# Attention and MoE on one core: turned-back products at 256 columns and an event table by name

## The chip, the cores and the metric

The kernel runs on one core of a Trainium2 chip. The metric is the time of one execution on the device, in microseconds; the median of several executions counts. The engines that matter here are TensorE (PE, with its weight loads shown apart as PEld), VectorE (DVE), ScalarE (ACT), GpSimd (POOL) and the queue of SyncE (SP), which issues most transfers.

## What is computed

Eight batches of eight heads go through rotary attention (576 positions, head width 64), and the 4608 resulting rows of width 512 go through a layer of eight experts of which each row uses one. All data are float32.

```python
q_rot, k_rot = rotate(q), rotate(k)              # B, H, S, D = 8, 8, 576, 64
scores = q_rot @ k_rot.T / sqrt(D)
attn = exp(scores - max(scores))
x = (attn / (sum(attn) + 1e-9)) @ v              # then heads side by side: 4608 x 512
e_idx = argmax(x @ w_gate); gate_w = softmax(x @ w_gate)[e_idx]
eom = sigmoid(x @ w_output_gate)
out[rows of e] = gate_w * eom[e] * (relu(x @ w1[e]) @ w2[e])
```

## The kernel before

**The pairs.** Two heads of one batch make a pair, four pairs a batch, 32 pairs in all. A pair takes nine steps; its step number is g = 9n + k for pair n. The raw and rotated queries and keys are split in a high and a low part (POOL multiplies, adds and subtracts, ACT rounds), because scores are made of three products each: high by high, high by low, low by high. The table UNITS puts the nine score tiles of a pair on five of its steps: tiles 0 and 1 on step 0, 2 and 3 on step 2, tile 4 (the last 64 queries of both heads, block-diagonal, `bd`) on step 4, 5 and 6 on step 5, 7 and 8 on step 7. In a unit of two, the first tile belongs to one head and the second to the other, so one reads the upper 64 partitions and the other the lower 64.

**A tile's way.** TensorE makes the scores of a tile (L496, six products). VectorE takes the maximum (L501), ScalarE the exponential with its sum (L514), VectorE turns the result in blocks of 32 (L521, 1152 columns for two tiles). After the last tile, the values are multiplied (L542, in the four pieces av0 to av3 of PIECES, spread between the score units of the next pair) and summed in the PSUM tile `acc`. ScalarE copies `acc` out (L549 to L551), TensorE multiplies it back into token rows by a matrix that holds the identity and the gate weights (`back`, L557, 160 columns for each of five chunks of tokens), and `divide` scales by one over the softmax sum into the row buffer `xb`: three VectorE operations (L565, L567, L570) and two ScalarE ones (L574). The score tiles hold two buffers of two PSUM banks, `acc` the other four banks; `acc` has one buffer. So av0 of a pair can start when `divide` of the pair before it has read `acc`.

**The order.** It is written by hand. EVENTS gives each event a step, counted from the pair's first, and a sub-slot within the step; `step` (L339) emits scores, maxima and exponentials of the step's unit and then the events of sub-slots 1, 2 and 3. Each engine runs its instructions in the order in which they are emitted. After the fourth pair of a batch, `place` spreads the routing of the batch's 576 tokens over the following 38 steps (offset PLACE = 20): sums of the logits (L603), the rank product (L682, L683: which place in its expert's list each token gets) into a free corner of `acc`, its readers on VectorE (L687 and the next), one-hot rows (L713 on VectorE, L715 on POOL), the list product (L723) into a corner of `acc` and its addition to the lists (L726), and three row stores from `xb` to `xd` in memory (L665, L667).

**The transfers.** SP issues the loads of queries and keys (`raw`, L426, two for a pair), of the values (`v`, L433: four of 32 partitions each for a pair, the same memory four times), the row stores and the weight loads (`wr`, L984). A load waits on its queue until the last reader of its buffer is done.

**The second part.** Slots of expert rows follow: gather (L971), turn (L1009), first product (L1023, L1031), second product (L1074), scatter. Slot 0's weights are loaded, and its first products made, while the last pairs still run.

## Time and profile before

| | us |
|---|---|
| median of three runs | 1078.68 |
| lowest and highest | 1078.12 and 1080.76 |
| the profiled execution | 1082.95 |
| its span, first to last instruction | 1081.0 |
| TensorE busy in the span | 995.4 |
| VectorE busy | 836.2 |
| ScalarE busy | 627.4 |
| GpSimd busy | 585.5 |

The profiled execution is 4.3 us longer than the median, and 1.9 us of it lie around the span. Times within the trace are microseconds from the span's start. The granted clock is the share of TensorE's full speed that the chip allowed in a stretch. "Idle before" is the time in which an engine stood still just ahead of an instruction, and the name behind the arrow is what ended last of what it waited for; "issue" means that nothing in the profile was waited for. TensorE overlaps products of its queue, so that a run of products is best read by the times at which they start.

### The profile page before, as it was taken

The numbers are of one execution on the slowest core, as the hardware profiler recorded it, in microseconds if no ns is written. First come the engines' busy times: TensorE is split into PE (matmuls) and PEld (weight loads), VectorE is DVE, ScalarE is ACT, GpSimd is POOL, SyncE is SP. The second block draws the span as 40 slices with busy tenths as digits, with TensorE's granted clock in tenths as the row PEclk, the third lists the DMA queues.
The fourth block names the chain that finished last, engine by engine and source line by source line (L and its number), as shares of the span: only waits on it lengthen the run. The fifth ranks groups of instructions, "written<-read, shape, count | busy, mean of one in ns | idle before, by whom it ended". The sixth has DMA issues, their size and how long they took to land.

```text
span 1081.0 us, 34609 instructions
## 1 busy us (share of the span) xinstructions
PE 995.4 (92%) x14465; PEld 864.7 (80%) x14465; DVE 836.2 (77%) x1364; ACT 627.4 (58%) x1318; POOL 585.5 (54%) x540
## 2 busy tenths in 40 slices
PE   4999999989999899999778999999999999999995
PEld 3888777777777777777667888889898898899984
DVE  6789898978989888887875787666867857767782
ACT  4566656646656565564444455545865856757762
POOL 5676796867968679586531242213542443542621
PEclk9999999989999998898889999999999999999998
DMA  6755574655746556455256597766977977888860
GB/s 196 191 149 139 159 215 119 174 141 152 209 115 183 158 137 198 113 162 149 52 162 200 181 340 220 248 214 203 342 231 265 325 261 266 310 300 280 270 254 28
DMA packets 59760, 216.47 MB, mean 200 GB/s; under 512 B 9453, under 2 KB 11596, under 8 KB 55504
## 3 DMA queue, kind: packets, MB, share of 16 engines
q1 hardware_dynamic: 51920, 194.41, 58.5%
q0 software_dynamic: 6496, 18.92, 4.9%
q8 instruction: 115, 1.88, 0.7%
q10 hardware_dynamic: 1184, 0.89, 0.3%
q14 instruction: 45, 0.37, 0.1%
HBM read 196.04 MB, written 20.24 MB: 200 GB/s over the span
## 4 chain that ended last, share of the span: by engine, by line
PE 73%; DVE 14%; issue 6%; ACT 3%; DMA 2%; POOL 1%; ACTq 0%; DVEq 0%; POOLq 0%
PE py L1074 17%; PE acc L542 17%; PE sc L496 16%; PE ph L1031 14%; PE ph L1023 5%; DVE m L501 4%; DVE pt L521 3%; DVE wl L995 2%; PE mtp L1009 1%; PE acc L557 1%; ACT pm L514 1%; DVE xb L565 1%; ACT xb L574 1%; PE acc L723 1%; PE htp L1059 1%
## 5 line engine op out<-in xcount | busy, mean ns | idle before, releaser
L514 ACT ACTIVATE pm<-sc,m 128x576 f32<-128x576 f32 x288 | 211.0, 737 | 191.3 <-DVE m L501 188.8
L995 DVE TENSOR_TENSOR wl<-wr,wh 128x1024 fp32r<-128x1024 f32 x183 | 254.4, 1402 | 50.5 <-ACT wh L993 48.7
L501 DVE TENSOR_REDUCE m<-sc 128x1 f32<-128x576 f32 x288 | 205.7, 748 | 74.8 <-PE sc L496 73.8
L542 PE MATMUL acc<-pt,v 32*64 32x128 f32 (+1 forms) x9216 | 213.9, 311 | 32.1 <-ACT xb L574 11.1
L496 PE MATMUL sc<-kh,q 64*128 64x288 f32 x1024 | 210.3, 332 | 21.2 <-ACT q L412 10.9
L542 PEld LDWEIGHTS acc<-pt,v 32*64 32x64 f32 x9216 | 171.2, 139 | 57.7 <-issue 28.8
L993 ACT CAST wh<-wr 128x1024 fp32r<-128x1024 f32 x208 | 212.7, 1051 | 5.9 <-DMA wr<-in_w 5.9
L1074 PE MATMUL py<-wh,ht 128*128 128x512 f32 x640 | 214.7, 400 | 0.0
L496 PEld LDWEIGHTS sc<-kh,q 64*128 64x128 f32 x1024 | 150.0, 195 | 54.6 <-ACT pm L514 27.1
L521 DVE STREAM_TRANSPOSE pt<-pm 128x1152 f32<-128x1152 f32 x128 | 174.6, 1364 | 0.0
L438 POOL TENSOR_TENSOR raw<-raw,rt 128x1152 f32<-128x1152 f32 x62 | 163.9, 2643 | 0.3
L1031 PE MATMUL ph<-xt,wh 128*128 128x256 f32 x896 | 161.6, 282 | 2.3 <-DVE xt L1012 1.0
L1031 PEld LDWEIGHTS ph<-xt,wh 128*128 128x128 f32 x896 | 138.5, 189 | 5.3 <-DVE xt L1012 1.9
L496 PE MATMUL sc<-kl,q 64*128 64x288 f32 x512 | 139.9, 304 | 0.0
L1074 PEld LDWEIGHTS py<-wh,ht 128*128 128x128 f32 x640 | 120.4, 188 | 24.0
L1031 PE MATMUL ph<-xt,wl 128*128 128x256 f32 x448 | 125.8, 281 | 0.0
L1074 PE MATMUL py<-wl,ht 128*128 128x512 f32 x320 | 125.1, 391 | 0.0
L995 POOL TENSOR_TENSOR wl<-wr,wh 128x1024 fp32r<-128x1024 f32 x25 | 62.0, 2480 | 111.4 <-ACT wh L993 97.6
L496 PEld LDWEIGHTS sc<-kl,q 64*128 64x128 f32 x512 | 96.8, 196 | 0.0
L442 POOL TENSOR_TENSOR raw<-raw 128x576 f32<-128x576 f32 x62 | 88.0, 1420 | 3.0
L420 POOL TENSOR_TENSOR kl<-raw,kh 128x576 fp32r<-128x576 f32 x31 | 43.7, 1411 | 81.7 <-ACT kh L412 72.1
L1031 PEld LDWEIGHTS ph<-xt,wl 128*128 128x128 f32 x448 | 84.6, 189 | 0.0
(247 smaller groups left out, 1358.7 us busy)
## 6 DMA issues: line engine op xcount, KB each, us to landing
wr<-in_w SPq DMA_DIRECT2D x208, 512.0 KB, 5.5
v<-in_v SPq DMA_DIRECT2D x128, 288.0 KB, 5.9
raw<-in_qk SPq DMA_DIRECT2D x62, 576.0 KB, 4.9
xd<-xb SPq DMA_DIRECT2D x16, 513.0 KB, 6.7
xd<-xb SPq DMA_DIRECT2D x8, 128.2 KB, 4.8
raw<-in_qk SPq DMA_DIRECT2D x2, 288.0 KB, 4.2
rt<-in_rope ACTq DMA_DIRECT2D x2, 288.0 KB, 4.0
raw<-in_qk SPq DMA_DIRECT2D x1, 320.0 KB, 6.7
```

The lines of the kernel that those rows point to most:

```text
L438: self.eng(eng).tensor_tensor(out=rv, in0=rv, in1=self.rt[:, 2 * t:2 * t + 2, x], op=ALU.mult)
L442: self.eng(eng).tensor_tensor(out=r[:, 2 * t, x], in0=r[:, 2 * t, x], in1=r[:, 2 * t + 1, x], op=ALU.add)
L496: nc.tensor.matmul(self.ps[i][:, a, :HS], st, mv, start=(n == 0), stop=(n == 2))
L501: nc.vector.tensor_reduce(self.m[i], ps[:, :, :HS], axis=AX.XY, op=ALU.max, negate=True)
L514: nc.scalar.activation(pe.rearrange("p (a b) -> p a b", a=2), self.ps[i][:, :, :HS], AF.Exp, bias=self.m[i], scale=1.0, accum_out=self.z[: ...
L521: self.nc.vector.transpose(out=self.pt[:, st[0]:st[0] + 6:5, :], in_=pe)
L542: nc.tensor.matmul(self.acc[h * D:h * D + D, a, o:o + 32 * n], self.v[r, h, j, :], self.pt[r, u:u + n, 32 * j:32 * j + 32], start=(j == 0) ...
L993: self.nc.scalar.copy(wh, r)
L995: eng.tensor_tensor(out=wl, in0=r, in1=wh.bitcast(F32), op=ALU.subtract)
L1023: nc.tensor.matmul(ph[:, 0, :], st[:, dc, 0:P], mv[:, dc, :], start=(n == 0), stop=(n == 11))
L1031: nc.tensor.matmul(ph[:, f, :], st[:, dc, fs], mv[:, dc, :], start=(n == 0), stop=(n == 11))
L1074: self.nc.tensor.matmul(py[h], st[:, f, hs], mv, start=(f == 0 and n == 0), stop=(f == 7 and n == 2))
```

## The change

Seven things change.

- **Score tiles in order.** OVER goes from 2 to 0: the second tile's six products follow the first tile's six, where before its first two were interleaved with the first tile's last two.
- **back and divide.** The five products of `back` lie at a spacing of 256 columns in three of `acc`'s banks, where before chunk c lay in bank c modulo 4. `divide` is then two VectorE operations over all five chunks; the third VectorE operation and both of ScalarE's go. The rank product and the list product go to the fourth bank, right behind `back` and ahead of the next scores; their readers on VectorE stand right behind `divide`.
- **den.** The copy of the last chunk's reciprocal goes from VectorE to POOL, and a memset of the row buffer's unused rows goes.
- **The event table.** EVENTS and the new PLACES name each step's place one by one; `step` has a sub-slot before the scores and one between scores and maxima. The query's low part and `lasts` come earlier; the rank product moves by two steps, one-hot rows are spread over steps 44 to 53 of the batch's last pair, the row stores over steps 45, 51 and 56 (before 51, 53 and 54).
- **Loads.** `raw` becomes two tiles. `v` is laid out in memory four times over, so that one transfer fills a head's 128 partitions: two of 576 KB for a pair where four of 288 KB stood. A POOL memset of one column stands ahead of the query load and of the second `v` load, so that these wait for their place in POOL's order.
- **Row stores.** Those of the last batch but one go into the list that the second part works off, and the last batch's go to the end of it.
- **Slot buffers.** At the end of attention only the first weight block of slot 0 is loaded at once, three more follow step by step, the gather of slot 1 comes later, and the turning buffers of the second part get four PSUM banks where they had two.

The diff, cut to its core:

```diff
-PIECES = ((0, 5), (5, 9), (9, 14), (14, 18))
-PLACE, PM = 20, 4
+BS = 256
+EVENTS = {
+    "load1": (-21, 3), "load0": (-16, 2), "mult1": (-11, 3), "add1": (-10, 1), "mult0": (-9, 0), "kh": (-9, 4),
+    "kl": (-6, 3), "add0": (-7, 2), "qh": (-4, 0), "ql": (-4, 2), "lasts": (-3, 2), "loadv0": (5, 4),
+    "loadv1": (6, 1), "av0": (12, 3), "av1": (13, 4), "av2": (14, 2), "av3": (17, 0), "den": (16, 0),
+    "evict": (17, 0), "newxb": (12, 4), "back": (18, 2), "divide": (18, 3),
+}
+PIECES = ((0, 5), (5, 9), (9, 13), (13, 18))
...
-UNITS, OVER = {0: (0, 1), 2: (2, 3), 4: (4,), 5: (5, 6), 7: (7, 8)}, 2
+UNITS, OVER = {0: (0, 1), 2: (2, 3), 4: (4,), 5: (5, 6), 7: (7, 8)}, 0
...
+        moe.load(3, 1)
         for u in range(1, 3):
             moe.split(u)
         att.rest(lambda g: g <= att.G + 8)
-        for j in range(2):
-            moe.products(0, j)
+        moe.products(0, 0)
         moe.first(0, 0)
+        att.rest(lambda g: g <= att.G + 10)
+        moe.products(0, 1)
         moe.first(0, 1)
...
+    small.move(turns, pool(ctx, "ps_y", 2, space=PSUM, side="left", reuse_waits="tile"))
...
+                        if b == nb - 2 and name in ("t0", "t1", "t2"):
+                            self.late.append(fs[name])
...
+            if self.n > 1:
+                self.nc.gpsimd.memset(self.raw[0][:, 0, 0:1], 0.0)
+        self.nc.sync.dma_start(out=self.raw[t], in_=self.qkd[:, 2 * t:2 * t + 2, :])
...
-        for a in (2 * t, 2 * t + 1):
-            self.nc.sync.dma_start(out=self.v[32 * a:32 * a + 32], in_=self.vd)
+        else:
+            self.nc.gpsimd.memset(self.v[:, t, 0, 0:1], 0.0)
+        self.nc.sync.dma_start(out=self.v[:, t, :, :], in_=self.vd[:, t, :, :])
...
-        V.tensor_scalar(rz[0:D, 9:10], rz[D:P, 8:9], 1.0, 0.0, op0=ALU.mult, op1=ALU.add, accum_out=no[0:D])
+        self.nc.gpsimd.tensor_copy(rz[0:D, 9:10], rz[D:P, 8:9])
...
+        self.bk = self.acc.rearrange("p a b -> p (a b)")
         for c in range(NCH):
-            n, o = (P, PO) if c < 4 else (QR, PO + BW)
-            self.nc.tensor.matmul(self.acc[0:n, c % 4, o:o + BW], self.ac[:, c, :, :].rearrange("p a x -> p (a x)")[:, 0:n],
+            n = P if c < 4 else QR
+            self.nc.tensor.matmul(self.bk[0:n, c * BS:c * BS + BW], self.ac[:, c, :, :].rearrange("p a x -> p (a x)")[:, 0:n],
...
-        V.tensor_tensor(out=heads(xb[:, 0:4, x0:x0 + P], D), in0=heads(acc[:, :, PO:PO + P], D),
-                        in1=r4.broadcast_to((P, 4, 2, D)), op=ALU.mult)
...
-        for h in range(2):
-            nc.scalar.activation(xb[0:QR, 4, x0 + h * D:x0 + h * D + D], last[:, h * D:h * D + D], AF.Copy,
-                                 scale=rz[0:QR, 8 + h:9 + h])
+        five = self.bk[:, 0:NCH * BS].rearrange("p (c x) -> p c x", c=NCH)
+        V.tensor_tensor(out=heads(xb[:, :, x0:x0 + P], D), in0=heads(five[:, :, 0:P], D), in1=r.broadcast_to((P, NCH, 2, D)), op=ALU.mult)
+        V.tensor_tensor(out=heads(xb[:, :, l0:l0 + 2 * HL], HL), in0=heads(five[:, :, P:BW], HL),
+                        in1=r.broadcast_to((P, NCH, 2, HL)), op=ALU.mult)
...
-        rk = T["rk"] = psum(2, 2, (NCH + 1) * E).rearrange("p (a b) -> p a b", b=E)
+        rk = T["rk"] = psum(2, 3, (NCH + 1) * E).rearrange("p (a b) -> p a b", b=E)
...
-        T["ls"] = psum(4, 1, lists.shape[1])
+        T["ls"] = psum(4, 3, lists.shape[1])
...
-    vl = np.ascontiguousarray(vr.reshape(nb, NP, 2, NB, 32, D).transpose(0, 1, 4, 2, 3, 5))
+    vl = np.ascontiguousarray(np.tile(vr.reshape(nb, NP, 2, NB, 32, D).transpose(0, 1, 4, 2, 3, 5), (1, 1, 4, 1, 1, 1)))
```

**TensorE at the first scores of pair 11** (`sc11` are its score tiles, `acc9` the tile in which pair 9 is turned back, `acc10` that of pair 10, whose values come next; L682 and L683 make the rank product of batch 1). Before:

```order
L496 MATMUL sc11_2_3270<-kl11_3029,q11_3081 128x288
L496 MATMUL sc11_3_3271<-kh11_3028,q11_3081 128x288
L496 MATMUL sc11_2_3270<-kh11_3028,q11_3081 128x288
L496 MATMUL sc11_3_3271<-kl11_3029,q11_3081 128x288
L496 MATMUL sc11_3_3271<-kh11_3028,q11_3081 128x288 x2
L496 MATMUL sc11_3_3271<-kl11_3029,q11_3081 128x288
L496 MATMUL sc11_3_3271<-kh11_3028,q11_3081 128x288
L682 LDWEIGHTS oneb_103
L682 MATMUL acc9_2987<-ohs1_3159,oneb_103 128x48
L683 LDWEIGHTS trib_102
L683 MATMUL acc9_2987<-ohb1_3155,trib_102 128x40
L542 MATMUL acc10_3298<-pt10_2922,v10_3152 64x160
```

After, from the products of `back` (L593) on:

```order
L593 MATMUL acc9_2974<-ii_102,ac9_3211 128x160 x4
L593 MATMUL acc9_2974<-ii_102,ac9_3211 64x160
L713 LDWEIGHTS oneb_104
L713 MATMUL acc9_2974<-ohs1_3130,oneb_104 128x48
L714 LDWEIGHTS trib_103
L714 MATMUL acc9_2974<-ohb1_3126,trib_103 128x40
L531 MATMUL sc11_2_3263<-kh11_2945,q11_3064 128x288
L531 MATMUL sc11_2_3263<-kl11_2946,q11_3064 128x288
L531 MATMUL sc11_2_3263<-kh11_2945,q11_3064 128x288 x2
L531 MATMUL sc11_2_3263<-kl11_2946,q11_3064 128x288
L531 MATMUL sc11_2_3263<-kh11_2945,q11_3064 128x288
L531 MATMUL sc11_3_3264<-kh11_2945,q11_3064 128x288
```

The rank product went from between the scores and the values to behind `back`; the scores of tile 2 end before those of tile 3 begin.

**VectorE at the same place** (`m` are the maxima of score tiles, `xb2` the row buffer). Before:

```order
L521 STREAM_TRANSPOSE pt10_2922<-pm10_7_3178 128x2x576
L565 TENSOR_TENSOR xb2_2944<-acc9_2987,rz1_117 128x4x128
L567 TENSOR_TENSOR xb2_2944<-acc9_2987,rz1_117 128x4x32
L570 TENSOR_TENSOR xb2_2944<-acc9_2987,rz1_117 64x32
L501 TENSOR_REDUCE m11_2_3285<-sc11_2_3270 128x1
L501 TENSOR_REDUCE m11_3_3288<-sc11_3_3271 128x1
L687 TENSOR_TENSOR pr1_3293<-acc9_2987,base1_3230 128x40
```

After:

```order
L556 STREAM_TRANSPOSE pt10_2910<-pm10_7_3162 128x2x576
L603 TENSOR_TENSOR xb2_2724<-acc9_2974,rz1_118 128x5x128
L604 TENSOR_TENSOR xb2_2724<-acc9_2974,rz1_118 128x5x32
L718 TENSOR_TENSOR pr1_3260<-acc9_2974,base1_3216 128x40
L719 TENSOR_TENSOR cnt_105<-acc9_2974,cnt_105 128x8
L536 TENSOR_REDUCE m11_2_3278<-sc11_2_3263 128x1
L536 TENSOR_REDUCE m11_3_3281<-sc11_3_3264 128x1
```

Two operations read the turned-back products where three did, and the rank product's readers (`pr1`, `cnt`) went from behind two maxima to ahead of them.

**SP's queue while the row stores of batch 1 are issued** (pairs 12 and 13 are being worked; `rk` and `rq` are the two tiles of `raw`). Before:

```order
L433 DMA v11_3461<-in_v 32x2304 x4
L426 DMA raw14_3560<-in_qk 128x1152 x2
L433 DMA v12_3769<-in_v 32x2304 x2
L665 DMA xd_83<-xb1_1726 128x2x513
L433 DMA v12_3769<-in_v 32x2304 x2
L665 DMA xd_83<-xb1_1726 128x2x513
L426 DMA raw15_3860<-in_qk 128x1152
L667 DMA xd_83<-xb1_1726 64x513
L426 DMA raw15_3860<-in_qk 128x1152
L433 DMA v13_4070<-in_v 32x2304 x4
```

After:

```order
L468 DMA v11_3435<-in_v 128x1152 x2
L460 DMA rk14_3441<-in_qk 128x1152
L696 DMA xd_83<-xb1_1513 128x2x513
L460 DMA rq14_3587<-in_qk 128x1152
L468 DMA v12_3738<-in_v 128x1152
L696 DMA xd_83<-xb1_1513 128x2x513
L468 DMA v12_3738<-in_v 128x1152
L460 DMA rk15_3746<-in_qk 128x1152
L698 DMA xd_83<-xb1_1513 64x513
L460 DMA rq15_3887<-in_qk 128x1152
L468 DMA v13_4039<-in_v 128x1152 x2
```

The three stores were one load apart and are now two loads apart, and the load of a pair's values went from four pieces to two, which no longer stand side by side.

## Rows read from the trace of the kernel before

**Rows 1.** The page: busy time of TensorE, and its granted clock in 40 slices.

```profile
PE 995.4 (92%) x14465; PEld 864.7 (80%) x14465; DVE 836.2 (77%) x1364; ACT 627.4 (58%) x1318; POOL 585.5 (54%) x540
...
PEclk9999999989999998898889999999999999999998
```

**Rows 2.** Busy times by stretch, one pair each: length, PE, PEld, DVE, ACT, POOL, clock, DMA.

```profile
63.68:78.86 15.18, 14.50 (x354) 12.32 (x353) 13.47 (x23) 9.93 (x28) 10.85 (x7) 1.00 0.56 141
...
190.35:206.47 16.12, 14.71 (x356) 12.45 (x355) 13.83 (x27) 10.04 (x29) 13.10 (x15) 1.00 0.54 137
206.47:225.48 19.01, 16.43 (x357) 13.60 (x355) 15.48 (x33) 10.30 (x29) 18.54 (x19) 0.91 0.75 205
225.48:244.95 19.47, 18.13 (x356) 15.19 (x355) 15.35 (x26) 9.71 (x28) 9.11 (x9) 0.82 0.46 123
```

**Rows 3.** Busy times by stretch: one batch, four, the last; the passage; the experts.

```profile
141.09:206.47 65.38, 60.07 (x1417) 50.02 (x1416) 58.35 (x109) 39.96 (x111) 52.61 (x57) 1.00 0.60 164
206.47:481.18 274.71, 252.56 (x5662) 210.82 (x5661) 234.02 (x433) 160.17 (x441) 210.31 (x225) 0.94 0.58 159
481.18:564.20 83.02, 69.71 (x1412) 57.42 (x1410) 64.14 (x134) 38.10 (x106) 43.80 (x57) 0.86 0.46 125
...
564.20:640.00 75.80, 67.47 (x683) 58.99 (x675) 53.73 (x113) 35.72 (x57) 22.73 (x21) 0.98 0.68 230
640.00:1045.00 405.00, 402.51 (x2653) 365.45 (x2653) 296.03 (x378) 258.44 (x368) 150.30 (x92) 1.00 0.80 271
```

**Rows 4.** Timeline at a divide: start, length, instruction, idle before and releaser.

```profile
66.31 0.65 DVE L565 TENSOR_TENSOR xb<-acc,rz 128x512 f32<-128x512 f32 x1
66.88 0.28 DVE L567 TENSOR_TENSOR xb<-acc,rz 128x128 f32<-128x128 f32 x1
67.08 0.17 DVE L570 TENSOR_TENSOR xb<-acc,rz 64x32 f32<-64x32 f32 x1
...
67.34 0.51 ACT L574 ACTIVATE xb<-acc,rz 64x64 f32<-64x64 f32 x2 [1.26 <-DVE xb L570]
...
67.90 1.64 PE L542 MATMUL acc<-pt,v 32*64 32x160 f32 x80 [0.68 <-DVE m L501]
```

**Rows 5.** Timeline of TensorE: first and last scores of tile 4, and of two tiles.

```profile
69.47 0.40 PE L496 MATMUL sc<-kh,bd 128*128 128x288 f32 x1
...
70.23 0.29 PE L496 MATMUL sc<-kh,bd 128*128 128x288 f32 x1
...
74.86 0.40 PE L496 MATMUL sc<-kh,q 64*128 64x288 f32 x1
...
76.24 0.28 PE L496 MATMUL sc<-kh,q 64*128 64x288 f32 x1
```

**Rows 6.** Waits of TensorE from 60 to 564 us: total us, times, longest.

```profile
PE acc L542 <- ACT xb L574: 10.4, 14, 1.5
PE acc L542 <- issue: 8.3, 7, 2.6
PE acc L542 <- PE acc L683: 5.1, 7, 0.7
...
PE acc L682 <- DVE m L501: 4.9, 7, 0.7
PE acc L542 <- DVE lists L726: 4.1, 6, 1.0
```

**Rows 7.** Timeline of TensorE: the second longest wait called issue.

```profile
219.68 0.77 PE L542 MATMUL acc<-pt,v 32*64 32x160 f32 x22 [1.81 <-issue]
```

**Rows 8.** Transfers: times issued, KB each, median us from issue to landing.

```profile
v<-in_v SPq DMA_DIRECT2D x128, 288.0 KB, 5.9
...
xd<-xb SPq DMA_DIRECT2D x16, 513.0 KB, 6.7
```

**Rows 9.** Timeline of POOL and of SP's queue in the pair of rows 4.

```profile
72.89 1.41 POOL L420 TENSOR_TENSOR q<-raw,q 128x576 fp32r<-128x576 f32 x1 [0.92 <-ACT q L412]
...
77.90 1.26 SPq L433 DMA_DIRECT2D v<-in_v  x3
```

More of the change, by code (lines that the diff above doesn't have):

```diff
@@ L197, in body @@
         moe.begin0()
+        for u in range(1, 3):
+            att.at(att.G + u - 1, 3, lambda u=u: moe.load(u, 1))
     for g in range(att.G, att.G + TURN):
@@ L200, in body @@
     scores.close()
-    small.move(pool(ctx, "ps_x", 2, space=PSUM, side="right", reuse_waits="tile"))
+    turns = pool(ctx, "ps_x", 2, space=PSUM, side="right", reuse_waits="tile")
+    small.move(turns)
     moe.ph = pool(ctx, "ps_h", 1, space=PSUM, side="right", reuse_waits="tile")
@@ L270, in __init__ @@
         self.go = px.tile([P, 1], F32, name="go")
-        self.last = []
+        self.last, self.late = [], []
         at = self.at
@@ L276, in newxb @@
             xbs[b] = px2.tile([P, NCH, RW], F32, tag="xb", name=f"xb{b}")
-            nc.gpsimd.memset(xbs[b][QR:P, NCH - 1, DM:], 0.0)
         for n, pr in enumerate(self.pairs):
@@ L292, in __init__ @@
                 fs[f"av{k}"] = lambda pr=pr, b0=b0, b1=b1: [pr.values(j) for j in range(b0, b1)]
-            for name, o, k in EVENTS:
+            for name, (o, k) in EVENTS.items():
+                if name in AFTER and g + EVENTS["back"][0] >= self.G:
+                    o, k = AFTER[name]
                 if n > 1 or name not in ("load1", "load0", "mult1", "add1", "kh", "kl", "mult0", "add0", "qh", "ql")[:10 if n == 0 else 2]:
@@ L299, in __init__ @@
                     self.last = fs
[L300 to L304 removed]
+                    for k, f in enumerate(self.late):
+                        self.last.insert(LATER + 2 * k, f)
+                else:
+                    for name, (o, k) in PLACES.items():
+                        if b == nb - 2 and name in ("t0", "t1", "t2"):
+                            self.late.append(fs[name])
                         else:
[L306 removed]
+                            at(g + o, k, fs[name])
     def done(self, b):
[L310 removed]
+        return 9 * (NP * b + NP - 1) + max(o for o, _ in PLACES.values()) + 2
     def at(self, g, k, f):
@@ L341, in step @@
         n, k = divmod(g, 9)
-        if g < G:
-            pr = pairs[n]
-            if k == 0:
-                pr.begin()
-            if k in UNITS:
-                pr.scores(UNITS[k])
-                pr.room(k)
-                for i in UNITS[k]:
-                    pr.peak(i)
-                    pr.exp(i)
-        self.now(g, 1)
+        self.now(g, 0)
+        unit = UNITS.get(k, ()) if g < G else ()
+        pr = pairs[n] if g < G else None
+        if pr and k == 0:
+            pr.begin()
+        if unit:
+            pr.scores(unit)
+        self.now(g, 1)
+        if unit:
+            pr.room(k)
+            for i in unit:
+                pr.peak(i)
+                pr.exp(i)
+        self.now(g, 2)
         if k in TURNS and 0 <= TURNS[k] + 9 * n < G:
@@ L355, in step @@
             pairs[i // 9].turn(i % 9)
-        self.now(g, 2)
         self.now(g, 3)
+        self.now(g, 4)
 class Pair:
@@ L973, in gather, with load @@
                 in_offset=bass.IndirectOffsetOnAxis(ap=self.ids(s, h), axis=0), bounds_check=n - 1, oob_is_err=False)
-    def load(self, u):
+    def load(self, u, late=0):
         if u >= 8 * self.end:
@@ L983, in load @@
         self.wr[u] = self.buf("wr", u, self.LOADS, 4, [P, 1024], F32, f"wr{u}{self.nm}")
+        if late == 1:
+            self.nc.vector.memset(self.wr[u][:, 0:1], 0.0)
+        elif late == 2:
+            self.nc.gpsimd.tensor_copy(self.wr[u][:, 0:1], self.wr[u - 2][:, 0:1])
         self.nc.sync.dma_start(out=self.wr[u], in_=self.w[bass.ds(self.regs[s] * P + j * E * P, P), :])
@@ L1096, in begin0 @@
             self.gather(s + 1)
-        for u in range(8 * s, 8 * s + 4):
+        for u in range(8 * s, 8 * s + 4 if end is not None else 8 * s + 1):
             self.load(u)
@@ L1109, in more @@
             if u not in self.wp and u not in self.wr:
-                self.load(u)
+                self.load(u, 2 * (s == 0 and u > 5))
         for u in range(8 * s + 3, 8 * s + self.LEAD):
```

105 lines of the change are left out of this document (49 added, 56 removed), and 9 rows, old and new, of tables (EVENTS, PLACES).

## The prediction

> **What bounds the kernel now.** I read the page first: TensorE is busy 92% of the span, no other engine above 77% [rows 1]. Next, busy time by stretch. The experts run at 402.51 us of 405.00 [rows 3], so nothing that the change does there can give more than some 2 us; the time to be had lies in attention. A pair without routing takes 15.18 us with TensorE busy for 14.50 [rows 2]: the missing 0.68 is one gap, ahead of the values, in every pair [rows 4]. Then the waits of TensorE by what ended them [rows 6], and last the granted clock: the first batches run at 1.00, four later ones at 0.94, the last at 0.86 [rows 3]. TensorE is the bound, and what can be won is its waits and its low clock; work taken from VectorE or ScalarE counts only where TensorE waits for it.
>
> The sum is made against the profiled 1082.95 us, 4.27 above the median of 1078.68; that difference is taken off at the end.
>
> **A. The wait for divide.** The values stand still for 0.68 us [rows 4]. The row names a maximum of VectorE, but 67.90 lies 0.05 behind the end of ScalarE's L574 (67.34 + 0.51 = 67.85), which is the last reader of `acc`, and the waits put 14 of these gaps to L574 [rows 6]. TensorE was thus done with the scores at 67.22. After, L574 and L570 are gone. The first new operation handles 640 columns where L565 takes 0.65 for 512, the second 160 where L567 takes 0.28 for 128: by columns at most 0.81 and 0.35, less if part of each is fixed. From starts (66.31, 66.88, 67.08) the pieces overlap by 0.08, so the reader ends at about 66.31 + 0.72 + 0.31 = 67.34 at the earliest and 67.40 at the latest: the values could start some 0.5 us earlier, and what is late then is the scores themselves (67.22, and later by part B). So 0.52 to 0.68 for each of 31 pairs, the gap whole if the scores run beyond 67.40: 0.6 x 31 = **-18.6**, bounds -16 and -21. The old third operation of `den` on VectorE, now a POOL copy, and the memset lie beside work of TensorE and give nothing.
>
> **B. Score tiles in order.** A unit of two tiles starts its first product at 74.86 and its last at 76.24: 1.38 us. A tile alone has 69.47 to 70.23, 0.76 [rows 5]. Two in a row take 0.76 + 0.76 and the step between them, 0 to 0.13 (a twelfth of the burst is 0.12): 1.52 to 1.65 if the second tile also begins with the slow first step, about 0.11 less if not. The loss is 0.03 to 0.27 a unit. I take 0.13, since the two tiles of a unit read different halves of the partitions, so the last product of the first and the first of the second can overlap as the interleaved ones did. Four units in each of 31 pairs: **+16.1**, bounds +4 and +33. So A and B nearly cancel in a plain pair, which should stay at 14.9 to 15.3 us.
>
> In the Trainium skill, TensorEngine Tiling (Array Packing), section Key Properties, it stands that tiles of the array operate independently and that different ones can load weights and multiply in parallel. This speaks against B: the interleave used it three times in a unit, tile by tile in order uses it once. By this rule alone the loss would be at its upper end, +33 in place of +16; the rows show 1.38 us for two tiles against 0.76 for one, which agrees with some overlap but not with two tiles at once.
>
> **C. Rank product.** It stands between scores and values, and the values wait 0.73 for it, 5.1 us in 7 times [rows 6]; its own wait ahead, 4.9 in 7, is part A's. Behind `back` the two products still take TensorE's time, but the values start after another unit of scores (1.4 us), and VectorE's two small readers fit under that. **-5**, bounds -3 and -6.
>
> **D. List product.** The values wait for L726, 4.1 us in 6 [rows 6]. After, the addition stands behind `divide`, and between `back` and the values lie the list products and 1.4 us of scores, longer than `divide` and the addition. **-4**, bounds -2 and -5.
>
> **E. Stalls and clock.** The waits called "issue" make 8.3 us in 7 [rows 6], one of them 1.81 us in the pair after a batch's end [rows 7], where stores, query loads and value loads are in flight together: DMA is 0.75 busy there, against 0.56 in a plain pair [rows 2]. Behind it the clock falls: 0.91 in that pair and 0.82 in the next, whose TensorE time is 18.13 against 14.50 though it does the same work [rows 2]. In these rows the lower clock (the 1.2 GHz level) comes behind such idle time. The four batches from 206.47 on take 274.71, against 4 x 65.38 = 261.52 for the batch at full clock: 13.2 more [rows 3]; in the last batch 0.14 x 83.02 = 11.6 us of clock are missing. Together 24.8. The change takes out the gap of every pair (A), C's and D's waits, spreads the stores and lets the value loads go in two pieces. The stalls themselves need not go, since as many instructions have to be supplied. I take three quarters: **-18**, bounds -7 and -25. This is the term that I know least.
>
> **F. Passage and experts.** In the passage TensorE is idle for 75.80 - 67.47 = 8.3 us [rows 3]; its divide waits go, its loads come later. **-3**, bounds -6 and 0. The experts get two more turning banks, for which at most 2.5 us of idle time are there: 0.
>
> **The loads.** Of the second half of `v`, the memset stands on POOL behind the query's low part, which ends at 72.89 + 1.41 = 74.30 [rows 9]; before, all of `v` was issued at about 77.90 for use a pair and more later. The values that need it begin one pair after 67.90, at 83.08. So the cover falls to 8.8 us. A landing takes 5.9 for half of such a piece and 6.7 for a store of 513 KB [rows 8]. In a plain pair this holds: 0. The other memsets only hold loads back that are used later: 0.
>
> **Sum.** -18.6 + 16.1 - 5 - 4 - 18 - 3 = -32.5: 1082.95 - 32.5 - 4.3 = about **1046**.
>
> **Rivals.**
> 1. *Stalls and clock stay.* The supply of instructions needs the same transfers, and in the pair after a batch's end they still meet stores. Then E is nothing: 1082.95 - 14.5 - 4.3 = 1064. For it: the stalls don't depend on the divide. Against: most low stretches follow several idle spells close to each other, and A, C and D take those away.
> 2. *The scores lose the whole overlap* (rule above): B at +33 gives 1063. If rivals 1 and 2 came together, 1081, no change.
> 3. *Slower: the values wait for their second half.* SP works in order, and in the pair after a batch's end a store of 513 KB goes just ahead of it (SP's queue after, above); POOL is busy 18.54 of 19.01 us there [rows 2], so the memset comes late too. The wait decides when landing exceeds 8.8 us: every us beyond costs 31 us if all pairs have it, 7 if only those. The gain of 32.5 is gone at 8.8 + 32.5/31 = 9.9 us. At 10.5 us, 53 lost: 1099. For it: 576 KB in one piece is more than anything the rows time at 5.9. Against: query loads of that size in a plain pair land in time, with DMA at 0.56; in the seven pairs alone a wait of 3 us costs 21, within my range.
> 4. *More gain.* B at its lower end and E whole: 1082.95 - 18.6 + 4 - 5 - 4 - 25 - 3 - 4.3 = 1027.
>
> **How the numbers follow.** Forecast (about 1034 to 1057) 0.53; rival 1 0.17; rival 2 0.07, and together with rival 1 0.04; rival 3 0.09; rival 4 0.10. The range runs from 1024 to 1069: it takes in rivals 1, 2 and most of 4, and leaves out rival 3, the double case and the end of rival 4, some 0.17. A measurement of this kernel can tell about 0.3%, 3.2 us, from no change. Faster by more: 0.53 + 0.17 + 0.07 + 0.10 = 0.87; within: 0.04; slower: 0.09.
>
> **What the profile after would show.** A: no idle time ahead of the first values of a pair, and L574 absent; a plain pair near 15.1 us. B: first to last score start of a unit at 1.4 to 1.65. C and D: no waits of the values for the rank product or the lists; the last pair of a batch near 15.5. E: clock 1.00 in nearly all slices, "issue" waits gone or shorter; if they stay at 8 us with clock 0.94, rival 1 holds. Rival 3 would be a wait of the values for a load of `v`, in all pairs or in every fourth. I am wrong in direction only if that wait, or another new one of over 1 us a pair, appears.

## The result, and the profile after

The changed kernel takes **1045.95 us** (median of four runs, 1043.49 to 1050.94) against 1079.72 of the kernel before (four runs, 1078.12 to 1082.61): ratio 0.969, 95% interval 0.9648 to 0.9732. The forecast was 1046. The profiled execution of the changed kernel is one of the four, 1043.49 us with a span of 1041.7; its span is 39.3 us shorter than that of the profile before, of which some 6 us are the choice of executions (that profile was above its median, this one is below).

The page of the changed kernel, with the lines that answer to [rows 1]:

```profile
PE 980.8 (94%) x14465; PEld 855.1 (82%) x14465; DVE 829.9 (80%) x1271; ACT 613.9 (59%) x1254; POOL 597.8 (57%) x642
...
PEclk9999999999999999999899999999999999999998
```

TensorE makes as many products in 15 us less busy time, mainly because the clock now falls in one slice of attention only. Busy time by stretch, columns as in [rows 2, 3]: a plain pair, then the four pairs behind a batch's end (the second has the list product, the fourth the rank product), then one batch, four batches, the last batch.

```profile
63.23:78.22 14.99, 14.76 (x354) 12.57 (x353) 13.44 (x19) 9.53 (x25) 11.11 (x10) 1.00 0.44 142
138.58:154.00 15.42, 14.74 (x354) 12.52 (x353) 15.01 (x28) 9.60 (x25) 15.19 (x16) 1.00 0.53 159
154.00:170.64 16.64, 15.74 (x359) 13.13 (x358) 15.02 (x22) 9.51 (x25) 12.64 (x14) 1.00 0.64 214
170.64:185.54 14.90, 14.66 (x354) 12.49 (x353) 13.72 (x23) 9.65 (x27) 13.33 (x23) 1.00 0.34 108
185.54:200.62 15.08, 14.71 (x356) 12.51 (x355) 14.21 (x26) 9.71 (x26) 12.68 (x20) 1.00 0.58 194
138.58:200.62 62.04, 59.85 (x1417) 50.65 (x1416) 57.95 (x97) 38.48 (x102) 53.84 (x70) 1.00 0.53 170
200.62:453.11 252.49, 241.38 (x5662) 202.82 (x5661) 231.88 (x384) 153.75 (x408) 215.67 (x277) 1.00 0.53 173
453.11:524.93 71.82, 63.59 (x1397) 52.43 (x1399) 63.18 (x119) 35.76 (x94) 44.19 (x66) 0.95 0.38 118
```

Beside [rows 3] this says where the 39.3 us went: 3.3 in the batch that ran at full clock before (65.38 to 62.04), 22.2 in the four batches behind it (274.71 to 252.49), 11.2 in the last (83.02 to 71.82), 2.5 in what comes ahead of them (141.09 to 138.58), and nothing behind attention: 1081.0 - 564.20 and 1041.7 - 524.93 are both 516.8.

The waits of TensorE from 60 to 564 us, as in [rows 6] (total, times, longest):

```profile
PE acc L577 <- PE sc L531: 8.3, 26, 0.5
PE sc L531 <- ACT pm L549: 8.3, 12, 3.7
PE acc L577 <- issue: 6.6, 12, 1.9
```

The waits for the rank product, the lists and ScalarE's L574 are gone. Ahead of the values stands a shorter wait, 8.3 us in 26 places, called one for the scores. The waits called issue make 6.6 us against 8.3, but this window takes in some 40 us that now lie behind attention. Up to its end at 524.93 us they are

```profile
PE acc L577 <- issue: 4.1, 8, 1.0
```

half of what they were, and the longest is 1.0 us where it was 2.6.

And the timeline at a divide, as in [rows 4]:

```profile
65.86 0.78 DVE L603 TENSOR_TENSOR xb<-acc,rz 128x640 f32<-128x640 f32 x1
66.57 0.30 DVE L604 TENSOR_TENSOR xb<-acc,rz 128x160 f32<-128x160 f32 x1
...
66.98 1.83 PE L577 MATMUL acc<-pt,v 32*64 32x160 f32 x80 [0.23 <-PE sc L531]
```

The second operation ends at 66.57 + 0.30 = 66.87 and the values start 0.11 later; ahead of them TensorE is idle for 0.23 where it was 0.68. The scores named in the row had ended 0.23 earlier. In the kernels of runs 3 and 7, too, the values start 0.10 behind the end of this operation. So divide is still what the values wait for, only for less long.

### The profile page after: what moved, and what is told of

Same layout as the page of the kernel before. It is cut to its first block, busy times and chain, and to the rows that moved or that the text cites. A ratio compares the mean times of both kernels' runs of the same rounds, so it can differ in the third digit from the quotient of the medians.

```text
span 1041.7 us, 34520 instructions
## 1 busy us (share of the span) xinstructions
PE 980.8 (94%) x14465; PEld 855.1 (82%) x14465; DVE 829.9 (80%) x1271; ACT 613.9 (59%) x1254; POOL 597.8 (57%) x642
## 4 chain that ended last, share of the span: by engine, by line
PE 73%; DVE 11%; issue 7%; ACT 4%; DMA 3%; POOL 1%; ACTq 0%; POOLq 0%; SPq 0%; DVEq 0%
PE sc L531 18%; PE acc L577 15%; PE py L1103 14%; PE ph L1060 14%; PE acc L593 5%; PE ph L1052 4%; DVE m L536 3%; DVE wl L1024 2%; DVE pt L556 2%; ACT wh L1022 2%; ACT pm L549 2%; DMA wr<-in_w 1%; PE mtp L1038 1%; DVE lgs L633 1%; PE acc L754 1%
## 5 line engine op out<-in xcount | busy, mean ns | idle before, releaser
L536 DVE TENSOR_REDUCE m<-sc 128x1 f32<-128x576 f32 x288 | 208.0, 752 | 45.6 <-PE sc L531 44.6
L577 PE MATMUL acc<-pt,v 32*64 32x128 f32 (+1 forms) x9216 | 203.1, 296 | 15.7 <-PE sc L531 8.5
L577 PEld LDWEIGHTS acc<-pt,v 32*64 32x64 f32 x9216 | 162.2, 132 | 42.2 <-issue 26.4
L531 PEld LDWEIGHTS sc<-kh,q 64*128 64x128 f32 x1024 | 152.8, 191 | 51.7 <-ACT pm L549 24.9
L531 PE MATMUL sc<-kl,q 64*128 64x288 f32 x512 | 132.3, 300 | 0.0
L1077 ACT ACTIVATE ht<-ph 128x512 fp32r<-128x512 f32 x56 | 33.5, 598 | 92.1 <-PE ph L1060 90.4
L531 PEld LDWEIGHTS sc<-kl,q 64*128 64x128 f32 x512 | 87.3, 193 | 0.0
L473 POOL TENSOR_TENSOR rk<-rk,rt 128x1152 f32<-128x1152 f32 x31 | 82.0, 2646 | 1.8
L1078 DVE SCALAR_TENSOR_TENSOR ht<-ph,ht 128x512 fp32r<-128x512 f32 x56 | 38.7, 691 | 55.0 <-ACT ht L1077 55.0
```

The lines of the kernel that those rows point to most:

```text
L473: self.eng(eng).tensor_tensor(out=rv, in0=rv, in1=self.rt[:, 2 * t:2 * t + 2, x], op=ALU.mult)
L531: nc.tensor.matmul(self.ps[i][:, a, :HS], st, mv, start=(n == 0), stop=(n == 2))
L536: nc.vector.tensor_reduce(self.m[i], ps[:, :, :HS], axis=AX.XY, op=ALU.max, negate=True)
L577: nc.tensor.matmul(self.acc[h * D:h * D + D, a, o:o + 32 * n], self.v[r, h, j, :], self.pt[r, u:u + n, 32 * j:32 * j + 32], start=(j == 0) ...
```

## The experiments

Three questions were open after the result: whether the order of score tiles costs anything (term B), what the shorter divide is worth by itself (A), and what keeps the clock up (E): the gaps of all pairs, the waits for the routing products (C and D), the places of the stores, or the loads. Runs 1 to 4 were timed on one chip beside the kernel before, whose median there was 1081.06 us; runs 5 to 8 on a second chip (1079.07), runs 9 to 12 on a third (1075.51). Comparisons between these groups therefore go by the ratio to it. Its mean granted clock was 0.973, 0.975 and 0.9775 there in the median of the executions; that of the changed kernel was 0.9875. Every kernel does the whole computation.

**1. Score tiles in order, on the kernel before.**

```diff
-UNITS, OVER = {0: (0, 1), 2: (2, 3), 4: (4,), 5: (5, 6), 7: (7, 8)}, 2
+UNITS, OVER = {0: (0, 1), 2: (2, 3), 4: (4,), 5: (5, 6), 7: (7, 8)}, 0
```

> The kernel before with one number changed: the second score tile of a unit follows the first (OVER 0). By term B of the prediction each unit that is not covered by the wait for divide loses 0.13 us: three units in 31 pairs, +12, about 1091; if the interleave was the only source of overlap, 0.27 each, +25, about 1104. Rival, from the trace after, where two tiles in order take 1.15 to 1.48 us from first to last start: the overlap is set by when a score buffer comes free and not by the order in the queue, so the time stays within 4 us of before, 1075 to 1083.

Measured: 1081.54 us, ratio 0.9996 (0.9959 to 1.0033). The order has no weight; the rival holds. A loss of 12 us would be a ratio of 1.011. The traces show why. Here is the unit of tiles 7 and 8 with the exponential that frees the second tile's buffer, first in the kernel before, then in this run:

```profile
74.60 0.73 ACT L514 ACTIVATE pm<-sc,m 128x576 f32<-128x576 f32 x1
75.23 0.64 PE L496 MATMUL sc<-kh,q 64*128 64x288 f32 x3
...
73.97 0.73 ACT L514 ACTIVATE pm<-sc,m 128x576 f32<-128x576 f32 x1
74.60 0.64 PE L496 MATMUL sc<-kh,q 64*128 64x288 f32 x3
```

The third product of each PE row is the second tile's first. It starts at 75.48 and 74.84, in both orders 0.62 us behind the first tile's first product and 0.04 behind the exponential's semaphore (75.43 and 74.80). From first to last start this unit takes 1.39 us in both orders (median over the pairs at full clock), the unit of tiles 5 and 6 1.32 interleaved and 1.31 in order, that of tiles 0 and 1 1.41 and 1.42. Only the unit of tiles 2 and 3 shows the 0.13 us of term B, 1.02 against 1.15, and behind it the values wait for divide anyway.

**2. The interleave put back, on the changed kernel.** The same line the other way round.

> The changed kernel with the interleave of score tiles put back (OVER 2). Term B at its value: 16 us less than the changed kernel, about 1030, and 1013 by the full loss. Rival, order without weight: 1041 to 1051, as the changed kernel.

Measured: 1041.5 us, ratio 0.9623 (0.9556 to 0.9689), beside 0.969 for the changed kernel. Not the 16 us of term B; a gain of some us isn't excluded. (Run 10 took it up again.) The trace of the changed kernel shows that tiles in order overlap as well. TensorE's timeline at the unit of tiles 0 and 1:

```profile
77.13 0.40 PE L531 MATMUL sc<-kh,q 64*128 64x288 f32 x1
77.37 0.29 PE L531 MATMUL sc<-kl,q 64*128 64x288 f32 x1
77.50 0.42 PE L531 MATMUL sc<-kh,q 64*128 64x288 f32 x3
77.75 0.31 PE L531 MATMUL sc<-kl,q 64*128 64x288 f32 x2
77.88 0.42 PE L531 MATMUL sc<-kh,q 64*128 64x288 f32 x3
```

A row gives the busy length of its products and not the time of each start. One by one, the fourth product starts at 77.51, 0.01 behind the third. By its length, 0.40 us like that of the first product of every tile, it is the second tile's first; the trace doesn't name the tile. It starts 0.38 behind the first tile's first product, and ahead of three products of the first tile that stand before it in the queue (77.64, 77.75 and 77.88). The twelve starts take 1.15 us here; the medians over the pairs at full clock are 1.15 in the changed kernel and 1.06 in this run for tiles 0 and 1, and 1.15 and 1.24 for tiles 2 and 3.

**3. Only the new divide, on the kernel before.** `back` and `divide` are those of the changed kernel; the list product goes to the fourth bank.

```diff
-            n, o = (P, PO) if c < 4 else (QR, PO + BW)
-            self.nc.tensor.matmul(self.acc[0:n, c % 4, o:o + BW], ...
+            n = P if c < 4 else QR
+            self.nc.tensor.matmul(self.bk[0:n, c * BS:c * BS + BW], ...
...
-        T["ls"] = psum(4, 1, lists.shape[1])
+        T["ls"] = psum(4, 3, lists.shape[1])
```

> The kernel before with only the new back and divide (256 columns apart, two VectorE operations; the list product moved to the fourth bank so that the two don't meet). Term A alone: the wait of 0.68 us shrinks to about 0.2, 0.45 to 0.5 in 31 pairs, -15: 1064. If the gaps of all pairs are what lets the clock fall, the clock comes back too, a good part of 25 us: 1045 to 1055, mean clock 0.985 or more. Rival: stalls of instruction supply and the stores let the clock fall, so it stays near 0.97 and the time at 1062 to 1067.

Measured: 1064.8 us, ratio 0.9835 (0.9767 to 0.9903), mean clock 0.980 to 0.985 in its runs. That is the size of A, 16 us, but less than half of it comes from the gaps. The timeline, at the same place as [rows 4]:

```profile
66.92 0.54 PE L544 MATMUL acc<-pt,v 32*64 32x160 f32 x17 [0.19 <-PE sc L498]
```

A plain pair of the first batch takes 14.69 us there (63.17 to 77.86) against 15.18: 0.49 of it is gone, and 0.30 in later batches (14.88). Two pairs of each batch gain nothing. Here are the one with the rank product, which took 16.12 before [rows 2], and the first behind a batch's end, the latter once more as it was in the kernel before:

```profile
189.35:205.54 16.19, 14.70 (x356) 12.44 (x355) 13.90 (x25) 9.56 (x27) 13.30 (x15) 1.00 0.54 145
270.50:286.77 16.27, 15.37 (x354) 12.61 (x353) 15.55 (x31) 9.43 (x26) 15.87 (x18) 1.00 0.81 224
...
276.30:292.48 16.18, 15.04 (x354) 12.52 (x353) 15.49 (x33) 9.95 (x28) 15.79 (x18) 1.00 0.75 197
```

In the former the values wait for the rank product in place of divide; in the latter VectorE is busy for 15.5 us, more than TensorE. Of the waits called issue, 17.7 us in 20 places, 9.3 stand right behind the rank product, 1.33 in each of 7 pairs; 8.4 lie within a run of values, against 5.7 in the kernel before (60 to 545 us). The rest of the gain goes with the clock: 0.9815 in the median against 0.973, by that 0.0085 x 1081 = some 9 us, an estimate. So in the old order the divide is worth some 7 us by itself and brings back part of the clock.

**4. The old divide, on the changed kernel.** The same edit the other way round, with the memset of the row buffer's unused rows put back.

> The changed kernel with the old back and divide (three VectorE operations, two ScalarE ones, chunk c in bank c modulo 4). If the gap ahead of the values is what A says, 0.5 to 0.7 us come back in 31 pairs: 1061 to 1067 with the clock unchanged; if the gaps also let the clock fall, 1070 to 1080 with a mean clock near 0.97.

Measured: 1066.13 us, ratio 0.9884 (0.9843 to 0.9924), 1.9% above the changed kernel, 20 us. The mean clock stays at 0.981 to 0.992. A plain pair takes 15.36 us there (63.75 to 79.11) against 14.90, the pair with the rank product 15.97 (192.01 to 207.98) against 15.08: over 31 pairs, 7 of them with the rank product, that makes some 17 of the 20 us. So in the new order the gap costs its own length and little more; it isn't what lets the clock fall there.

```profile
67.97 0.49 PE L578 MATMUL acc<-pt,v 32*64 32x160 f32 x9 [0.71 <-DVE m L537]
```

This row of its timeline is the old wait, 0.71 us.

**5. The stores at the old steps, on the changed kernel.**

```diff
-    "o0": (44, 2), "o1": (49, 2), "o2": (50, 1), "o3": (51, 4), "o4": (53, 4), "t0": (45, 3),
-    "t1": (51, 1), "t2": (56, 0), "s20": (54, 3), "s21": (55, 4),
+    "o0": (44, 2), "o1": (49, 2), "o2": (50, 1), "o3": (51, 4), "o4": (53, 4), "t0": (51, 4),
+    "t1": (53, 4), "t2": (54, 4), "s20": (54, 3), "s21": (55, 4),
```

> The changed kernel with the row stores of a batch at the old steps (51, 53 and 54 in place of 45, 51 and 56). If the spread of the stores is what keeps the clock up, the waits called issue grow to 8 us and more, the mean clock falls to about 0.975 and the time rises by 8 to 15 us: 1054 to 1061. Rival: the stores don't matter, 1042 to 1050, clock 0.985 to 0.992.

Measured: 1044.2 us, ratio 0.9677 (0.9626 to 0.9729): no weight.

**6. The stores at the new steps, on the kernel before.**

```diff
-        fs[25] = s13
-        fs[31], fs[33] = lambda: store(0), lambda: store(1)
-        fs[34] = lambda: store(2)
+        fs[25] = lambda: (s13(), store(0))
+        fs[31] = lambda: store(1)
+        fs[36] = lambda: store(2)
```

> The kernel before with its row stores at the new steps (about 46, 51 and 56) and nothing else. If the stores make the stalls behind which the clock falls: clock 0.985, 10 to 15 us faster, 1066 to 1071. Rival: stalls and clock as before, 1078 to 1084.

Measured: 1092.91 us, ratio 1.0147 (1.0084 to 1.0211): slower, which neither theory had. Its waits of TensorE, 60 to 545 us:

```profile
PE acc L542 <- issue: 12.9, 7, 3.8
...
PE sc L496 <- issue: 2.8, 1, 2.8
...
PE acc L557 <- issue: 1.8, 1, 1.8
```

The stalls rose to 17.5 us and the clock fell to 0.965. So the places of the stores have weight in the old order. What they meet there was not tried apart.

**7. No memsets ahead of loads, on the changed kernel.**

```diff
-            if self.n > 1:
-                self.nc.gpsimd.memset(self.raw[0][:, 0, 0:1], 0.0)
...
-        else:
-            self.nc.gpsimd.memset(self.v[:, t, 0, 0:1], 0.0)
```

> The changed kernel without the POOL memsets that hold back the query load and the second half of the values: these are issued when SP comes to them. If the held-back loads keep transfers apart and so the clock up, 1050 to 1060 with a mean clock of 0.98 or less; rival 3 of the prediction, that the held-back values come late, would make it faster, 1036 to 1041. If neither, 1042 to 1050.

Measured: **1037.15 us** (1033.05 to 1039.55), ratio 0.9599 (0.9546 to 0.9653): faster than the kernel before, 0.9% below the changed one's ratio, and 7 us below run 5 on the same chip. So the held-back loads keep no clock up. No wait for a load of values is behind the gain: in the changed kernel TensorE has none. What its trace shows is the run of values behind divide:

```profile
66.51 1.62 PE L573 MATMUL acc<-pt,v 32*64 32x160 f32 x80 [0.22 <-PE sc L527]
68.06 0.40 PE L527 MATMUL sc<-kh,bd 128*128 128x288 f32 x1
```

These 80 products take 68.06 - 66.51 = 1.55 us, as in all pairs of this run that don't stall. In the changed kernel they take 68.74 - 66.98 = 1.76 in the pair shown, 1.67 in most pairs, and 1.55 in six. Where they take longer, the trace has an instruction in TensorE's queue behind the first product that does nothing but wait for a semaphore; without the memset there is none. A plain pair is 14.79 us long (62.77 to 77.56) where 14.90 is usual in the changed kernel: 0.11 us, in 31 pairs some 3.5. The same holds with the interleave (14.91 in run 2, 14.79 in run 10). The rest of the gain isn't explained, and may be no more than the clock's changes from one execution to the next: run 10, below, has the interleave and no memsets, and its ratio, 0.9634, is no better than the 0.9623 of run 2, which has both.

**8. The rank and list products behind `back`, on the kernel before.**

```diff
-                            at(g + PLACE + k + 1, 1, f)
+                            at(g + PLACE + k, 2, f[0])
+                            at(g + PLACE + k, 3, f[1])
...
-17: lambda: (s14(), s14b(), s9())
+17: (s14, lambda: (s14b(), s9()))
...
-35: lambda: (s20(), s21())
+35: (s20, s21)
```

> The kernel before with the rank product and the list product directly behind back, and their readers directly behind divide. By terms C and D the values no longer wait for them, 9 us: 1071. If those waits are also what lets the clock fall in the pairs behind the list product (most of the low stretches begin within such a pair), 8 to 15 us more: 1056 to 1063 and a mean clock of 0.985. Rival: the readers now lie ahead of the values and the wait only moves, 1078 to 1084.

Measured: 1077.18 us, ratio 0.9984 (0.9949 to 1.0019): nothing. VectorE's timeline shows where the wait went, right behind the old divide:

```profile
194.62 0.17 DVE L571 TENSOR_TENSOR xb<-acc,rz 64x32 f32<-64x32 f32 x1
195.49 0.20 DVE L688 TENSOR_TENSOR pr<-acc,base 128x40 f32<-128x40 f32 x1 [0.70 <-ACT xb L575]
```

The reader of the rank product waits 0.70 us on VectorE for ScalarE's part of the old divide, and the values, which need that reader, start at 196.01 after 1.12 us of idle time. (The profile calls this a wait for a load of values. The load that these values need had landed at 179.72; the name is that of the next load on the same semaphore, which was under way.) The pair is 0.4 us shorter than before, 15.75 (191.21 to 206.96) against 16.12, but the pair with the list product is longer, 17.71 (223.13 to 240.84) against 17.21 (157.99 to 175.20) in the kernel before. So C is worth little and D costs while ScalarE has a part in the divide.

**9. Both, on the kernel before** (the edits of 3 and 8).

> The kernel before with the new back and divide and with the rank and list products directly behind back, their readers directly behind divide. If C and D are hidden once divide is short (readers done before the scores that follow): 1064.8 less 9, 1056, with the clock at 0.985 or more. If they merely move the wait, as they did on the kernel before: 1062 to 1066. If the clock needs both, 1045 to 1052, which would leave nothing for the new event table and the loads.

Measured: 1058.96 us, ratio 0.9857 (0.981 to 0.9904), beside 0.9835 for the divide alone: no gain that can be told in the sum, although the pair with the rank product shrank from 16.2 us (189.35 to 205.54 in run 3). The pair with the list product grew. Here is the first of these in this run, then the second, in run 3 and in this run:

```profile
187.80:203.41 15.61, 14.63 (x356) 12.44 (x355) 14.00 (x26) 9.64 (x27) 13.30 (x15) 1.00 0.60 169
...
223.04:239.40 16.36, 15.63 (x359) 13.07 (x358) 15.26 (x24) 9.45 (x27) 10.18 (x9) 1.00 0.47 137
219.66:236.69 17.03, 15.95 (x359) 13.29 (x358) 15.27 (x24) 9.40 (x27) 11.36 (x9) 1.00 0.57 155
```

C gives 0.58 us a batch and D takes 0.67 back.

So some 1.5% of the 3.1% is had without the new event table and the new loads.

**10. No memsets, and interleaved.** The edits of 7 and 2.

> The changed kernel without the POOL memsets ahead of loads, and with the interleave of score tiles. If interleaving is worth the 4 us by which it stood under the changed kernel: 1032 to 1034. If the order of score tiles has no weight: 1035 to 1040, as without the memsets alone.

Measured: 1036.94 us, ratio 0.9634 (0.9593 to 0.9675): as without the memsets alone (0.9599). The order of the tiles has no weight here that can be told.

**11. No memsets, and the values in four pieces.** The edit of 7, and the values loaded as in the kernel before.

```diff
-        self.nc.sync.dma_start(out=self.v[:, t, :, :], in_=self.vd[:, t, :, :])
+        for a in (2 * t, 2 * t + 1):
+            self.nc.sync.dma_start(out=self.v[32 * a:32 * a + 32], in_=self.vd)
...
-    vl = np.ascontiguousarray(np.tile(vr.reshape(nb, NP, 2, NB, 32, D).transpose(0, 1, 4, 2, 3, 5), (1, 1, 4, 1, 1, 1)))
+    vl = np.ascontiguousarray(vr.reshape(nb, NP, 2, NB, 32, D).transpose(0, 1, 4, 2, 3, 5))
```

> The changed kernel without the POOL memsets and with the values loaded as before, in four pieces of 32 partitions for a pair. If the larger pieces are worth something (fewer issues, fewer stalls of instruction supply): 1042 to 1052 and more waits called issue. If not: 1034 to 1040.

Measured: 1070.13 us, ratio 0.9938 (0.9903 to 0.9972), 36 us by the ratios above run 7; mean clock 0.967 to 0.981 (0.974 in the median, 0.9895 in run 7). So in the new order the shape of the value loads is what E rests on. With it goes the memory that is read: four times the same 288 KB, or four copies; the two weren't tried apart. Waits and clock from 60 to 545 us, first of this kernel, then of run 7:

```profile
PE acc L574 <- issue: 19.3, 8, 5.2
60.00:545.00 485.00, 448.01 (x10066) 375.83 (x10060) 414.08 (x689) 274.32 (x728) 369.53 (x415) 0.95 0.59 152
...
PE acc L573 <- issue: 5.5, 5, 2.4
60.00:545.00 485.00, 459.33 (x10731) 388.19 (x10730) 439.22 (x740) 288.85 (x757) 382.41 (x434) 0.99 0.52 167
```

The waits are 14 us longer, and 0.04 x 485 = some 19 us of clock are missing: together most of the 36. A plain pair of this kernel, columns as in [rows 2]:

```profile
63.00:77.80 14.80, 14.56 (x354) 12.40 (x353) 13.43 (x20) 9.52 (x25) 11.06 (x8) 1.00 0.61 162
```

The longest pair behind a batch's end, and the longest stall within it:

```profile
357.15:383.68 26.53, 19.81 (x358) 16.02 (x357) 14.96 (x22) 9.21 (x24) 13.33 (x12) 0.74 0.65 162
367.80:373.00 5.20, 0.04 (x3) 0.00 (x0) 2.62 (x4) 1.39 (x3) 1.40 (x1) 0.66 1.01 221
```

And TensorE's timeline where that stall ends:

```profile
373.01 1.91 PE L574 MATMUL acc<-pt,v 32*64 32x160 f32 x48 [5.17 <-issue]
```

For 5.2 us the DMA engines are full (share 1.01) and TensorE stands in the middle of a run of products: in the trace the next packet of instructions (16 KB) begins only at 370.22 and takes 1.29 us, while some 40 value packets of 9216 bytes are under way in each microsecond. TensorE starts again 1.50 us behind the packet's end. This is so at every stall of over 0.25 us within a run of products from 60 to 545 us: the nine of this run end 1.24 to 1.50 us behind the end of such a packet, the six of the kernel before 1.30 to 1.56. So these stalls are waits for instructions; that full engines make the packets late is inferred. In the kernel before, too, value packets of 9216 bytes hold 0.49 to 0.62 of the engines' time around the late packet at the four longest of them (from 4 us ahead of it to its end), and row stores 0.34 to 0.45; here the value packets hold 0.52 to 0.86. In the 7 us behind the stall the granted clock is 0.52, nearly all of it at the lower level:

```profile
373.00:380.00 7.00, 6.99 (x126) 5.84 (x126) 2.38 (x6) 2.03 (x6) 0.68 (x3) 0.52 0.41 138
```

Beside this, the plain pair of run 7, with the same bytes a second:

```profile
62.77:77.56 14.79, 14.57 (x354) 12.42 (x353) 13.45 (x20) 9.54 (x25) 11.06 (x8) 1.00 0.49 162
```

Both move 162 GB/s, but the four pieces keep the DMA engines busy for 0.61 of the time and the two of 128 partitions for 0.49. By packets: one of 9216 bytes takes 0.66 us (median), one of 4608 bytes 0.18, four times as long for twice the bytes.

**12. The rank and list products at their old place, on the changed kernel.**

```diff
-"s14": (36, 3), "s14b": (37, 4)
+"s14": (38, 1), "s14b": (38, 2)
...
-"s20": (54, 3), "s21": (55, 4)
+"s20": (56, 1), "s21": (56, 2)
```

> The changed kernel with the rank and list products back between the second unit of scores and the values, their readers behind that unit's maxima. By C and D the waits of the values come back, 0.7 us in 13 places: 1055. If these waits also let the clock fall: 1060 to 1072 with a mean clock of 0.98 or less. If it has no weight: 1042 to 1050.

Measured: 1054.8 us, ratio 0.9789 (0.9741 to 0.9838), 1.0% above the changed kernel, as C and D say; mean clock 0.982 to 0.989. The pair with the rank product, by stretch, in two batches, and the pair with the list product:

```profile
188.03:205.88 17.85, 16.32 (x356) 13.85 (x355) 14.22 (x26) 9.72 (x26) 12.64 (x20) 0.90 0.48 164
253.32:269.73 16.41, 14.88 (x356) 12.62 (x355) 14.21 (x25) 9.73 (x26) 12.05 (x19) 1.00 0.48 162
...
221.28:237.75 16.47, 15.70 (x359) 13.14 (x358) 15.03 (x23) 9.53 (x25) 12.65 (x14) 1.00 0.66 214
```

16.41 against 15.08 us is 1.3 us a batch from the wait alone; where the clock fell with it, 2.8. All of that is the rank product's: the pair with the list product takes 16.47 us here and 16.44 in the changed kernel (216.04 to 232.48).

## Why the prediction held

The forecast, 1046, met 1045.95. The sum was right, and so was the mechanism in the main: shorter waits of TensorE and a higher clock. Of its six terms C with D had about the right size together, A had it in the new order only, E came out somewhat smaller, B was wrong, and F gave nothing.

- **A, -18.6.** Run 4 gives -20 in the new order. In the old order (run 3) the gain is 16 us, but the gaps make some 7 of it and the clock the rest. What I had wrong is what is late next. I took the scores to end last; divide still does, by the 0.23 us ahead of the values. So a plain pair keeps part of the gap.
- **B, +16.1.** This step failed. Run 1 has 0, runs 2 and 10 nothing that can be told. I derived the loss from one tile's 0.76 us and two tiles' 1.38 and took the order in the queue for the source of the overlap. The Trainium skill (TensorEngine Tiling (Array Packing), Key Properties) says that tiles operate independently; I read it as a rule against the change, as if only neighbours in the queue could overlap. The rows show two things in its place: in the units of tiles 5 and 6 and of 7 and 8 the second tile starts when its buffer comes free, 0.55 and 0.62 us behind the first in both orders; and where nothing holds it, it runs beside the first even when it is queued wholly behind it. Rival 2 is out.
- **The plain pair**, foretold at 14.9 to 15.3 us, is 14.99 and 14.90, but not by A against B. From the former: the wait and the unit ahead of it give 0.19 (1.98 to 1.79 us); the first unit gives 0.28 (1.64 us from its first start to the next work before, 1.36 now, 62.13 to 63.49), which no term had and which is not the divide's, since it takes 1.65 in run 3 and 1.36 in run 4; the unit of tiles 7 and 8 takes back 0.11 (1.60 to 1.71, interleaved or not) and the run of values behind the wait 0.19 here and 0.10 in most pairs (1.57 to 1.76 and 1.67), this through the memset of run 7, which I had put at nothing.
- **C and D, -9.** Run 12 puts them at 1.0%, some 10 us, in the new order. All of it is C, 7 x 1.33 = 9.3 where I had 5; D gave nothing of its 4. The values' wait for the lists is gone, but the pair is as long without it. They were written as if they stood by themselves: a batch gains 0.4 us by C with the old divide (run 8), 0.6 with the new one (run 9), 1.33 in the new order, and by D it loses 0.5 and 0.7 in the old order and 0 in the new.
- **E, -18.** Four batches now miss 252.49 - 4 x 62.04 = 4.3 us where 13.2 were missing, the last batch 0.05 x 71.82 = 3.6 us of clock where 11.6 were: -17. But one of these two profiles is above its kernel's median and the other below; by the medians of the mean clock (0.973 to 0.9775 before, 0.9875 after) it is 11 to 16 us, an estimate. The 4.3 us taken off at the end of the sum overlap with E, since executions of one kernel differ by their clock (of the kernel before, 1072.96 us at 0.982 and 1088.38 at 0.966 on one chip). That the stalls need not go held in part: 4.1 us in attention where 8.3 were. Of the reasons, the gaps count in the old order (run 3: 0.973 to 0.9815) and not in the new one (run 4: 0.985 against 0.9875); the stores don't matter in the new order (run 5) and harm in the old (run 6). In the new order the value loads do. I had named them last among E's reasons and put them at 0 in the paragraph on loads, where I asked only whether they come in time. Run 11 has 36 us for their shape (whether whole or in four pieces). How E divides between divide, table and loads on the way from the old kernel to the new one isn't shown.
- **F, -3.** Nothing: 516.8 us on both sides.
- **Rival 1** (stalls and clock stay) is out; run 11 is what it looks like, by another cause. **Rival 3** didn't come in its form: no wait for the values' second half stands in the trace. But the memset it hung on does cost, some 3.5 us within the pairs by run 7.

A and B together were put at -2.5 and gave -6 to -9 (0.19 and 0.28 us in two plain pairs, 31 times); C and D gave one more than their 9, E some 1 to 7 less than its 18, F three less. B's 16 us show so little in the sum because other errors met them: by the plain pair A's wait gave some 6 us of its 18.6, and the memsets and the unit of tiles 7 and 8 took some 3.5 each, while the first unit gave 9 that no term had. To that extent the agreement within a microsecond is luck. Rival 4 was nearer with B and further off with E. The parts undone one by one (20, 10 and, without the memsets, 36 us) add up to more than the 34 us of the whole, so they aren't independent: run 11, which has the new table, divide and products but the old shape of the value loads, is 0.8% slower by the ratios than run 9, which has the old table. The new order needs the new loads, at least without the memsets; with them, the old loads weren't tried. Whether the new loads alone would help the old order wasn't tried either.

## What to carry to other kernels

Loads that arrive in time can still cost: where TensorE stalls on "issue" and the DMA share is near 1, look at how long a packet holds an engine, and give one load all 128 partitions before moving it about in the program. The Trainium skill (DMA: Bandwidth & Descriptors, Rules for kernel authors) advises one transfer of 128 partitions in place of two to disjoint halves of them; this case agrees for quarters, with 36 us for it (run 11). And a part that is worth next to nothing alone may be worth its whole price once another wait is gone (runs 8 and 12), so undo parts from the finished kernel as well as adding them to the old one.

## What the runs showed of the hardware

- The packets of 9216 bytes to 32 partitions took 0.66 us each, those of 4608 bytes to 128 partitions 0.18: at the same 162 GB/s the DMA share was 0.61 and 0.49.
- TensorE's instructions come in packets of 16 KB through the same DMA engines. When such a packet was late, TensorE stood still in the middle of a run of products and started again 1.24 to 1.50 us behind the packet's end (run 11). With the engines full, it stood for up to 5.17 us, and in the 7 us behind that the granted clock was 0.52, next to the 1.2 GHz level.
- Products of two tiles on different halves of the partitions start beside each other although one tile's six are queued ahead of the other's (the second tile's first at 77.51, three of the first tile's from 77.64 on), so the trace's starts aren't the queue's order.
- A memset of one column, 0.10 us on POOL, ahead of a load cost TensorE 0.12 us in most pairs (1.67 against 1.55 for 80 products), through one more waiting instruction.
